# First input in one transfer, first weights sent for by ScalarE, and the second block joining at tile 12: the start of a fused attention and MoE kernel

## The chip, the cores and the metric

The kernel runs on one core of a Trainium2 chip. Its engines are TensorE (PE; PEld is its weight load), VectorE (DVE), ScalarE (ACT), GpSimd (POOL) and SyncE (SP, which here only issues transfers); transfers run on the core's 16 DMA engines. The metric is the device time of one execution in microseconds.

## The reference

Three layers run one after the other on 8192 tokens (two sequences of 4096) of 192 numbers. The first is an attention over the current and the six earlier tokens, with weights from a softmax over seven given numbers for each token and head; the others are two MoE layers with 2048 hidden columns.

```python
def _attn_ref(x, weight_gen):                  # x (2, 4096, 192), weight_gen (2, 4096, 8, 7)
    w = weight_gen - np.max(weight_gen, axis=-1, keepdims=True)
    w = np.exp(w)
    w = w / (np.sum(w, axis=-1, keepdims=True) + 1e-09)
    x_pad = np.concatenate([np.zeros((B, pad, D)), x], axis=1)
    idx = np.arange(S)[:, None] + np.arange(K)[None, :]
    x_unf = x_pad[:, idx, :].reshape(B, S, K, H, group)
    return np.einsum('bshk,bskhg->bshg', w, x_unf).reshape(B, S, D)

def _moe_ref(x, w_in, w_out):                  # w_in (192, 2048), w_out (2048, 192)
    h = np.maximum(x @ w_in, 0.0)
    return h * h @ w_out

def _moe2_ref(x, w_in, w_out):
    h = x @ w_in
    return (h * np.cos(h)) @ w_out
```

## The kernel before, in words

**Tiling.** The tokens are cut into 16 blocks of 512 (`N`), and the 2048 hidden columns of a layer into 16 tiles f of 128 (`NF`). A step (layer, block, tile) has five first products (L560), which make the tile `h`, and five second products (L577 to L583), which add it into two accumulators `acc`: ten matmuls with 512 columns each, since every fp32 operand is split into a high part and a low part that the PE can multiply at its faster rate. There are 512 steps and so 5120 products. Between the two kinds of product ACT and DVE (and POOL, later on) apply the layer's function to `h` and split it (`hi` L264, `lo` L271).

**Order of the steps.** The first layer's blocks 0 to 5 come first, then the two layers alternate by blocks. At the start block 0 runs alone for `ALONE` tiles (6); then blocks 0 and 1 alternate tile by tile, so that block 1's steps stand between the later tiles of block 0 (L538 to L541).

**Weights.** They arrive as fp32 and are split on the chip in pieces (`weight`, parts a and b for `w_in`, o for `w_out`): for each piece a load into a shared room (`wo_early` and others), an absolute value on ACT (L303), a scaled copy on POOL or ACT (L310), a sign mask on DVE (L313), a clamp on DVE or POOL (L315), a merge on DVE (L318), a sum on POOL (L320), then the copy to the high part (L264, L268) and the subtraction for the low part (L271). The names `wiAhi`, `wiAlo`, `wiB` and `wo` are the finished weights. The first layer's pieces are planned ahead of the step that needs them (`pace`).

**First block.** `load_x(0)` brings block 0's tokens as rows of 1920 numbers, a row for each partition, with the six tokens ahead of it: partitions 2 to 63 (62 rows) on SP's queue, 64 to 127 (64 rows) on ACT's; two short transfers fill partitions 0 and 1. `first_x1` then makes block 0's input for the MoE at once on PE: DVE multiplies a quarter of it with its seven weights (L441), PE sums the taps by seven matmuls with the identity (L482), DVE folds the last 64 columns in three additions (L487), PE transposes those (L493), and the sum is split (`xhi`, `xlo`). This is done four times, i = 0 to 3; the first two need the first half of the softmax (`wgen`, L402 to L414), the others the second.

**Other blocks.** POOL makes the four products (`pr`, L441), DVE reduces them (`at`, L454) and transposes them (L506), SP stores and reloads the result through DRAM (L512, L517), and it is split into `xhi` and `xlo` of that block, (0, 1) for block 1.

**What sets the order.** Every operation is recorded with the engines that could run it, a cost for each, what it reads and writes, and when it is due. `Order.issue` (L112 to L161) then hands them out greedily, engine by engine; the result is one fixed list of instructions for each engine, which the hardware runs in that order, an instruction waiting for what it needs. `SENT`, `RATE` and `SEEN` are the planner's own figures for a transfer, `since` a time before which it leaves an operation out of sight, `by` a time at which it is due, `behind` an operation that it is tied to. `WARM` matmuls with the identity (L700) run on PE before anything else.

Of the kernel before, what the change touches and what calls it, by code (L numbers as in the profile page):

```python
# [18 lines left out]
P = 128  # L19
# [4 lines left out]
LAG = 6  # L24
START = 18.0
LEAD = 6
ALONE = 6
WARM = 16


def bits(n):
# [24 lines left out]
class Order:  # L56
    WAIT = 0.14

    SENT, RATE, SEEN = 0.65, 360e3, 0.77

    MORE = {"dve": 0.6, "pool": 0.0, "act": 0.05}
    NEAR = 0.02
# [25 lines left out]
    def op(self, ways, fn, reads=(), writes=(), size=0, behind=None, by=1e9, over=(), since=0.0):  # L88
        o = Op()
        o.ways, o.fn, o.size = ways, fn, size  # L90
        o.late = self.SENT + size / self.RATE + self.SEEN if size else 0.0
        o.behind, o.by, o.since = behind, by, max(since, self.since)
        o.older, o.deps, o.after, o.n = set(over), set(), set(behind or ()), len(self.ops)
        for write, accesses in ((False, reads), (True, writes)):
            for a in accesses:
                b, key = a if isinstance(a, tuple) else (a, None)
                for p, w, k in b.log:
                    if (w or write) and (k is None or key is None or k == key):
                        o.deps.add(p)
                if b.log:  # L100
                    o.after.add(b.log[0][0])
                elif b.before is not None:
                    o.after.add(b.before.log[0][0])
                if b.older is not None:
                    o.older.add(b.older)
                b.log.append((o, write, key))
        o.deps.discard(o)
        o.after.discard(o)
        self.ops.append(o)
        return o  # L110
# [57 lines left out]
def dve(n, fast=False):  # L168
    return 0.069 + n / (1600 if fast else 900)
# [7 lines left out]
def conv_moe_kernel(  # L177
# [11 lines left out]
    B, S, D = x.shape  # L189
# [9 lines left out]
    DB = D - P  # L199
# [8 lines left out]
    w_in = [w.bitcast(U32) for w in (moe_w_in, moe2_w_in)]  # L208
# [5 lines left out]
    order = Order()  # L214
    op, buf = order.op, order.buf
# [5 lines left out]
    def const(shape, dtype, name):  # L221
        return Buf(None, tile=sb.tile(shape, dtype, name=name))

    def load(dst, out_fn, in_ap, size, key=None, reads=(), by=1e9, queue="sp"):
        op({queue: 0.45}, lambda e: eng[e].dma_start(out=out_fn(), in_=in_ap), reads=reads,
           writes=[(dst, key)], size=size, by=by)

    ident = const([P, P], F32, "ident")
    zero = const([P, 1], F32, "zero")
# [44 lines left out]
    def weight(m, part, c0, n):  # L274
        name = f"{part}{m}_{c0}"
        by = -99.0 if m == c0 == 0 and part != "o" else 1e9
        if m == 0:
            order.since = 3.0 if by < 0 else 5.0
        stage = lambda tag, n, shape: (
            order.lent(room[tag], tag + "0", f"{tag}{name}") if m == 0 else sbuf(shape, U32, tag, n, f"{tag}{name}"))  # L280
        raw = stage("raw", 2, [P, WC, 2])
        flat = lambda: raw.t.rearrange("p a b -> p (a b)")
        if part == "a":
            cols = n
            load(raw, lambda: flat()[:, 0:2 * n], w_in[m][0:P, 2 * c0:2 * (c0 + n)], P * n * 8, by=by)
        elif part == "b":

            cols = n // 2
            ap = w_in[m][P:D, 2 * c0:2 * (c0 + n)].rearrange("d (j k c) -> k d j c", k=2, c=2 * P)
            for k in range(2):  # L290
                load(raw, lambda k=k: flat()[k * DB:(k + 1) * DB, 0:n].rearrange("d (j c) -> d j c", c=2 * P),
                     ap[k], DB * n * 4, key=k, by=by)
        else:
            cols = n * D
            load(raw, lambda: flat()[:, 0:2 * n * D].rearrange("p (j d) -> p j d", j=n),
                 w_out[m][c0 * P:(c0 + n) * P, :].rearrange("(j p) d -> p j d", p=P), P * cols * 8)
# [64 lines left out]
    def load_x(b):  # L361
        rows = BS + PAD
        t = xc[b] = sbuf([P, rows, D], F32, "xc", 2, f"xc{b}")

        def rows_of(p0, p1, skip=0):
            ap = x_rows[b * N + p0 * BS - PAD + skip:b * N + p0 * BS + BS, :]
            return bass.AP(tensor=ap.tensor, offset=ap.offset, ap=[[BS * D, p1 - p0], [1, (rows - skip) * D]])


        p0 = -(-PAD // BS) if b * N % S == 0 else 0  # L370
        flat = lambda a, b, skip: t.t[a:b, skip:rows].rearrange("p r d -> p (r d)")
        if b:
            load(t, lambda: flat(p0, P, 0), rows_of(p0, P), P * rows * D * 4, key="all")
        else:
            for n, q in enumerate(((p0, P // 2), (P // 2, P))):
                load(t, lambda q=q: flat(*q, 0), rows_of(*q), P // 2 * rows * D * 4, key=f"all{n}", by=-100.0,
                     queue="act" if n else "sp")
        if p0:
            op({"pool": 1.0}, lambda e: nc.gpsimd.memset(t.t[0:p0, 0:PAD, :], 0.0), [], [(t, p) for p in range(1, p0)])
        for p in range(p0):  # L380
            skip = PAD - p * BS
            load(t, lambda p=p, skip=skip: flat(p, p + 1, skip), rows_of(p, p + 1, skip), 8192, key=p, by=1e9 if b else -100.0)
# [8 lines left out]
    exps = []  # L391
# [77 lines left out]
    def first_x1():  # L469
        t = [buf(ps, [P, N], F32, "h", 4, f"first{part}") for part in range(2)]  # L470
        for i in range(BS):
            if i < 2:
                pr = sbuf([P, K, D], F32, "pr", 2, f"pr0_{i}")
            else:
                pr = order.lent([pr0[:, i - 2]], f"pr{i}", f"pr0_{i}")
            twice = order.lent([twice0[:, i]], f"twice{i}", f"twice{i}")
            product(0, i, pr, ways={"dve": dve(K * D)})
            there = lambda part, i=i: t[part].t.rearrange("d (p i) -> d i p", i=BS)[:, i]

            def taps(e, pr=pr, there=there):  # L480
                for k in range(K):
                    nc.tensor.matmul(there(0), lhsT=pr.t[:, k, 0:P], rhs=ident.t, start=k == 0, stop=k == K - 1)  # L482
            op({"pe": 0.24 * K}, taps, [ident, (pr, 0)], [(t[0], i)])

            def fold(e, pr=pr, twice=twice):
                p = pr.t[:, :, P:D]
                add = lambda out, in0, in1: eng[e].tensor_tensor(out=out, in0=in0, in1=in1, op=ALU.add)  # L487
                add(p[:, 0:3], p[:, 0:3], p[:, 3:6])
                add(p[:, 0:2], p[:, 0:2], p[:, 2:7:4])
                add(twice.t, *(p[:, k].unsqueeze(1).to_broadcast([P, 2, DB]) for k in range(2)))  # L490
            op({"dve": dve(3 * DB) + 2 * dve(2 * DB)}, fold, [], [(pr, 1), twice])

            op({"pe": 0.24}, lambda e, twice=twice, there=there: nc.tensor.transpose(  # L493
                there(1), twice.t.rearrange("p q d -> p (q d)"), ident.t), [ident, twice], [(t[1], i)])
        for part in range(2):
            split((0, 0), part, t[part], True)
# [40 lines left out]

    two = steps[:ALONE]  # L538
    for f in range(NF - ALONE):
# [118 lines left out]
    for b in range(NB):  # L658
        when(final[0, b] + LAG + 1, take_x2, b)
        when(final[1, b] + LAG + 1, take_out, b)  # L660
        t = first[1, b]
# [3 lines left out]
        t = first[0, b]  # L665
        ago = lambda n: max(t - n, -1) if b > 1 else -1
        when(ago(NF + 8), load_x, b)
        if b % CB == 0:
# [4 lines left out]
            else:  # L673
                n = 14 + 9 * c
# [6 lines left out]
    t = first[1, 0]  # L681
# [69 lines left out]
```

## Time and profile before

| what | us |
|---|---|
| three runs | 1277.4, 1278.64, 1281.92 (median 1278.64) |
| the profiled execution | 1277.48 |
| its span, first to last instruction | 1274.5 |
| PE busy | 1196.8 |
| ACT busy | 1054.9 |
| DVE busy | 902.8 |
| POOL busy | 551.2 |

The span is what the trace covers; 2.98 us of the profiled execution lie around it. Busy is the time in which an engine had an instruction in hand; overlapping engines each count in full. A row of a timeline gives the start, the duration, the engine, the line and the operation, output from input, with the count at x; in brackets stands how long the engine was idle before it and what ended that.

### The profile page before, as it was taken

The numbers are of one execution on the slowest core, as the hardware profiler recorded it, in microseconds if no ns is written. First come the engines' busy times: TensorE is split into PE (matmuls) and PEld (weight loads), VectorE is DVE, ScalarE is ACT, GpSimd is POOL, SyncE is SP. The second block draws the span as 40 slices with busy tenths as digits, with TensorE's granted clock in tenths as the row PEclk, the third lists the DMA queues.
The fourth block names the chain that finished last, engine by engine and source line by source line (L and its number), as shares of the span: only waits on it lengthen the run. The fifth ranks groups of instructions, "written<-read, shape, count | busy, mean of one in ns | idle before, by whom it ended". The sixth has DMA issues, their size and how long they took to land.

```text
span 1274.5 us, 16270 instructions
## 1 busy us (share of the span) xinstructions
PE 1196.8 (94%) x5212; PEld 979.1 (77%) x5212; DVE 902.8 (71%) x1217; ACT 1054.9 (83%) x1992; POOL 551.2 (43%) x425
## 2 busy tenths in 40 slices
PE   4488999989999999999999999999999999999998
PEld 4367777778787887878788787878878888888886
DVE  5998879775958578585866758576674646777765
ACT  1486887869788797978879798888988979999996
POOL 3678465564615244260534526153332304444443
PEclk8689999999999999999999999999999999999999
DMA  4532435320212112021111202111020210111001
GB/s 115 154 96 67 133 109 166 113 69 21 80 30 69 25 31 79 10 72 31 56 46 28 74 9 69 34 37 27 24 47 9 54 30 13 30 30 30 13 7 19
DMA packets 91945, 68.67 MB, mean 54 GB/s; under 512 B 56020, under 2 KB 77268, under 8 KB 91860
## 3 DMA queue, kind: packets, MB, share of 16 engines
q1 hardware_dynamic: 91780, 67.16, 19.1%
q8 instruction: 40, 0.66, 0.2%
q10 hardware_dynamic: 80, 0.49, 0.2%
q14 instruction: 45, 0.37, 0.1%
HBM read 47.76 MB, written 19.86 MB: 53 GB/s over the span
## 4 chain that ended last, share of the span: by engine, by line
PE 50%; ACT 18%; DVE 14%; issue 5%; DMA 2%; POOL 1%; SPq 1%; DVEq 0%; ACTq 0%; POOLq 0%
PE h L560 25%; PE acc L579 5%; PE acc L577 5%; PE acc L578 5%; PE acc L582 5%; PE acc L583 5%; ACT hi L264 5%; DVE lo L271 4%; ACT rr L609 4%; ACT rr L610 4%; DVE g L612 2%; ACT kk L604 2%; DVE rr L607 2%; ACT g L598 2%; DVE at L454 1%
## 5 line engine op out<-in xcount | busy, mean ns | idle before, releaser
L271 POOL TENSOR_TENSOR lo<-g,hi 128x512 fp32r<-128x512 f32 x201 | 260.2, 1295 | 557.4 <-ACT hi L264 489.3
L271 DVE TENSOR_TENSOR lo<-g,hi 128x512 fp32r<-128x512 f32 x215 | 175.0, 814 | 157.1 <-ACT hi L264 147.5
L264 ACT ACTIVATE hi<-g 128x512 fp32r<-128x512 f32 x416 | 259.8, 625 | 1.9 <-DVE g L612 0.9
L607 DVE SCALAR_TENSOR_TENSOR rr<-kk,h 128x512 f32<-128x512 int32 x256 | 174.4, 681 | 90.0 <-ACT kk L604 90.0
L612 DVE TENSOR_TENSOR g<-h,rr 128x512 f32<-128x512 f32 x256 | 175.0, 684 | 38.6 <-POOL lo L271 26.8
L577 PE MATMUL acc<-hi,wo 128*128 128x512 f32 x512 | 200.3, 391 | 1.5 <-ACT wo L264 1.5
L578 PE MATMUL acc<-hi,wo 128*128 128x512 f32 x512 | 200.6, 392 | 1.0 <-DVE wo L271 1.0
L582 PE MATMUL acc<-lo,wo 128*128 128x512 f32 x512 | 200.4, 391 | 0.0
L579 PE MATMUL acc<-hi,wo 128*128 128x512 f32 x512 | 200.4, 391 | 0.0
L583 PE MATMUL acc<-lo,wo 128*128 128x512 f32 x512 | 200.2, 391 | 0.0
L594 ACT ACTIVATE rr<-h 128x512 f32<-128x512 f32 x256 | 150.7, 590 | 51.0 <-PE h L560 50.0
L609 ACT ACTIVATE rr<-rr 128x512 f32<-128x512 f32 x256 | 161.1, 629 | 27.7 <-DVE rr L607 27.4
L610 ACT ACTIVATE rr<-rr 128x512 f32<-128x512 f32 x256 | 161.2, 630 | 1.8
L604 ACT ACTIVATE kk<-h 128x512 int32<-128x512 f32 x256 | 151.1, 590 | 8.5 <-PE h L560 7.8
L598 ACT ACTIVATE g<-rr 128x512 f32<-128x512 f32 x160 | 100.7, 630 | 55.1 <-DVE lo L271 51.5
L441 POOL TENSOR_TENSOR pr<-xc,wgen_late 128x1344 f32<-128x1344 f32 x48 | 139.5, 2984 | 13.2 <-DVE at L454 11.8
L577 PEld LDWEIGHTS acc<-hi,wo 128*128 128x128 f32 x512 | 96.8, 189 | 22.1 <-ACT wo L264 1.9
L578 PEld LDWEIGHTS acc<-hi,wo 128*128 128x128 f32 x512 | 96.7, 189 | 21.6 <-DVE wo L271 1.3
L582 PEld LDWEIGHTS acc<-lo,wo 128*128 128x128 f32 x512 | 96.7, 189 | 20.3
L583 PEld LDWEIGHTS acc<-lo,wo 128*128 128x128 f32 x512 | 96.8, 189 | 20.1
L579 PEld LDWEIGHTS acc<-hi,wo 128*128 128x128 f32 x512 | 96.8, 189 | 20.0
L454 DVE TENSOR_REDUCE at<-pr 128x192 f32<-128x1344 f32 x60 | 92.3, 1539 | 0.0
(558 smaller groups left out, 2243.7 us busy)
## 6 DMA issues: line engine op xcount, KB each, us to landing
xc<-in_x_dram SPq DMA_DIRECT2D x14, 960.0 KB, 4.7
x2d<-x2a SPq DMA_DIRECT2D x16, 256.0 KB, 2.0
x<-x2d SPq DMA_DIRECT2D x32, 128.0 KB, 2.7
x<-x2d SPq DMA_DIRECT2D x16, 256.0 KB, 2.7
out_dram<-oa SPq DMA_DIRECT2D x64, 64.0 KB, 2.0
x1d<-xt SPq DMA_DIRECT2D x60, 64.0 KB, 1.8
x<-x1d SPq DMA_DIRECT2D x15, 256.0 KB, 2.7
x<-x1d SPq DMA_DIRECT2D x30, 128.0 KB, 2.6
```

The source lines that it names most:

```text
L264: nc.scalar.activation(out, in_, AF.Copy)
L271: eng[e].tensor_tensor(out=out, in0=in0, in1=in1, op=ALU.subtract)
L560: nc.tensor.matmul(h.t, lhsT=w.t[:, sl], rhs=v.t, start=n == 0, stop=n == len(ops) - 1)
L577: nc.tensor.matmul(o0.t, lhsT=w(0), rhs=hi.t, start=start, stop=False)
L578: nc.tensor.matmul(o1.t, lhsT=w(2), rhs=hi.t, start=start, stop=False)
L579: nc.tensor.matmul(o0.t, lhsT=w(1), rhs=hi.t, start=False, stop=False)
L582: nc.tensor.matmul(o1.t, lhsT=w(2), rhs=lo.t, start=False, stop=stop)
L583: nc.tensor.matmul(o0.t, lhsT=w(0), rhs=lo.t, start=False, stop=stop)
L607: op({"dve": dve(N)}, lambda e: nc.vector.scalar_tensor_tensor(out=r.t, in0=k.t, scalar=-TWO_PI, in1=h.t, op0=ALU.mult, op1=ALU.add), [k, ...
L609: op({"act": act(N)}, lambda e: nc.scalar.activation(r.t, r.t, AF.Abs), [], [r])
L610: op({"act": act(N)}, lambda e: nc.scalar.activation(r.t, r.t, AF.Sin, scale=-1.0, bias=math.pi / 2), [], [r], behind=exps if (b, f) == (0 ...
L612: op({"dve": dve(N)}, lambda e: nc.vector.tensor_tensor(out=g.t, in0=h.t, in1=r.t, op=ALU.mult), [h, r], [g])
```

## The change

The first input's 126 rows come in one transfer on SP, where there were two of 62 and 64 rows on two queues. The first pieces of the first layer's weights are issued on ACT's queue and tied to the first exponential. Blocks 0 and 1 alternate from tile 12 on instead of 6, which moves much in the lists of DVE, POOL and SP. Ten more warm-up matmuls are issued, and the planner's figures for a transfer, its cost of a fold and some `since` values change.

```diff
-ALONE = 6
-WARM = 16
+ALONE = 12
+WARM = 26
...
-    SENT, RATE, SEEN = 0.65, 360e3, 0.77
+    SENT, RATE, SEEN = 0.75, 300e3, 0.8
...
-    def load(dst, out_fn, in_ap, size, key=None, reads=(), by=1e9, queue="sp"):
+    def load(dst, out_fn, in_ap, size, key=None, reads=(), by=1e9, queue="sp", behind=None):
         op({queue: 0.45}, lambda e: eng[e].dma_start(out=out_fn(), in_=in_ap), reads=reads,
-           writes=[(dst, key)], size=size, by=by)
+           writes=[(dst, key)], size=size, by=by, behind=behind)
...
         by = -99.0 if m == c0 == 0 and part != "o" else 1e9
+
+        early = dict(queue="act", behind=exps[:1], by=by) if by < 0 else {}
         if m == 0:
-            order.since = 3.0 if by < 0 else 5.0
+            order.since = 0.0 if by < 0 else 6.5
...
-            load(raw, lambda: flat()[:, 0:2 * n], w_in[m][0:P, 2 * c0:2 * (c0 + n)], P * n * 8, by=by)
+            load(raw, lambda: flat()[:, 0:2 * n], w_in[m][0:P, 2 * c0:2 * (c0 + n)], P * n * 8, **early)
...
-                     ap[k], DB * n * 4, key=k, by=by)
+                     ap[k], DB * n * 4, key=k, **early)
...
-        if b:
-            load(t, lambda: flat(p0, P, 0), rows_of(p0, P), P * rows * D * 4, key="all")
-        else:
-            for n, q in enumerate(((p0, P // 2), (P // 2, P))):
-                load(t, lambda q=q: flat(*q, 0), rows_of(*q), P // 2 * rows * D * 4, key=f"all{n}", by=-100.0,
-                     queue="act" if n else "sp")
+        if b == 1:
+            order.since = 6.5
+        load(t, lambda: flat(p0, P, 0), rows_of(p0, P), P * rows * D * 4, key="all", by=1e9 if b else -100.0)
+        order.since = 0.0
...
-            op({"dve": dve(3 * DB) + 2 * dve(2 * DB)}, fold, [], [(pr, 1), twice])
+            op({"dve": 1.0}, fold, [], [(pr, 1), twice])
```

Line numbers from L280 to L371 are two higher after the change (L313 becomes L315, L318 becomes L320); the others named here stay.

The start of SP's list, as a piece of the difference; `xc` is a block's input, `wgen` the softmax weights, and the transfers are given as rows by columns:

```order
-L225 DMA wgen_99<-in_weight_gen_dram 128x224
-L225 DMA xc_101<-in_x_dram 62x1920
-L225 DMA xc_101<-in_x_dram 1x768
-L225 DMA xc_101<-in_x_dram 1x1536
-L225 DMA wgen_99<-in_weight_gen_dram 128x224
-L225 DMA xc_108<-in_x_dram 128x1920
-L225 DMA wgen_112<-in_weight_gen_dram 128x224
-L225 DMA wo_early<-in_moe_w_in_dram 128x512
-L225 DMA wo_early<-in_moe_w_in_dram 64x2x256 x2
-L225 DMA wgen_112<-in_weight_gen_dram 128x224
+L225 DMA wgen_109<-in_weight_gen_dram 128x224
+L225 DMA xc_111<-in_x_dram 126x1920
```

The 64-row half, which stood on ACT's queue, is gone; the first weights (128x512, and 64x2x256 twice) have left SP for ACT, and block 1's input (`xc_108`) goes down the list behind the weights that follow.

The list of DVE of the kernel before, from the third product of `first_x1` to the split of block 0's input, which the first product needs; `at1` is block 1's attention, `wo1_early` also the room in which `first_x1` works:

```order
L441 TENSOR_TENSOR wo1_early_72<-xc0_101,wgen0_99 128x1344 x2
...
L454 TENSOR_REDUCE at1_200<-pr1_0_174 128x192
L313 TENSOR_SCALAR wiB1_early_70<-wo1_early_72 128x256 x2
...
L318 SCALAR_TENSOR_TENSOR wiB1_early_70<-wiAlo1_early_68,wiB1_early_70 128x256 x2
L454 TENSOR_REDUCE at1_200<-pr1_1_198 128x192
L313 TENSOR_SCALAR wiB1_early_70<-wo1_early_72 128x384
L315 TENSOR_SCALAR wiAlo1_early_68<-wiAlo1_early_68 128x384
L271 TENSOR_TENSOR xlo0_(0, 0)_224<-first0_132,xhi0_(0, 0)_203 128x512
```

The same place after the change:

```order
L441 TENSOR_TENSOR wo1_early_72<-xc0_111,wgen0_109 128x1344
...
L487 TENSOR_TENSOR wo1_early_72<-wo1_early_72 128x128
L315 TENSOR_SCALAR wiB1_early_70<-wo1_early_72 128x256 x2
L320 SCALAR_TENSOR_TENSOR wiB1_early_70<-wiAlo1_early_68,wiB1_early_70 128x256 x2
L315 TENSOR_SCALAR wiB1_early_70<-wo1_early_72 128x384
L271 TENSOR_TENSOR xlo0_(0, 0)_215<-first0_139,xhi0_(0, 0)_202 128x512
```

Block 1's two reductions have moved behind the split, and so has the second half of the softmax (which stood ahead of the rows shown). On POOL block 1's four products stand as instructions 15 to 18 before, right behind five short weight passes, and as 28, 29, 34 and 35 after.

The list of PE where block 1's first tile joins, before (`xlo0_(0, 1)` is block 1's input, `xlo0_(0, 0)` block 0's):

```order
L560 MATMUL h7_412<-xlo0_(0, 1)_370,wiAhi0_65 128x512
L560 MATMUL h7_412<-xhi0_(0, 1)_359,wiAlo0_67 128x512
L560 MATMUL h7_412<-xhi0_(0, 1)_359,wiAhi0_65 128x512
L560 MATMUL h7_412<-xlo1_(0, 1)_400,wiB0_69 128x512
L560 MATMUL h7_412<-xhi1_(0, 1)_388,wiB0_69 128x512
L560 MATMUL h8_427<-xlo0_(0, 0)_224,wiAhi0_65 128x512
```

and after:

```order
L560 MATMUL h13_646<-xlo0_(0, 1)_583,wiAhi0_65 128x512
L560 MATMUL h13_646<-xhi0_(0, 1)_577,wiAlo0_67 128x512
L560 MATMUL h13_646<-xhi0_(0, 1)_577,wiAhi0_65 128x512
L560 MATMUL h13_646<-xlo1_(0, 1)_636,wiB0_69 128x512
L560 MATMUL h13_646<-xhi1_(0, 1)_627,wiB0_69 128x512
L560 MATMUL h14_657<-xlo0_(0, 0)_215,wiAhi0_65 128x512
```

Block 1's first tile moved from the 8th step, behind 45 products, to the 14th, behind 115. Step h14 is tile 13 of block 0: it stands behind 120 products here and behind 170 in the list before, where it is step h20.

## Rows read from the trace of the kernel before

**Rows 1.** The page: busy us of each engine, share of the span, instructions.

```profile
PE 1196.8 (94%) x5212; PEld 979.1 (77%) x5212; DVE 902.8 (71%) x1217; ACT 1054.9 (83%) x1992; POOL 551.2 (43%) x425
```

**Rows 2.** Windows by stage: from and to, length, busy us of each engine (instructions).

```profile
core 0: us, PE busy (x) PEld busy (x) DVE busy (x) ACT busy (x) POOL busy (x), PEclk, DMA share, GB/s
0.00:17.60 17.60, 5.57 (x32) 5.38 (x32) 2.21 (x8) 1.87 (x3) 1.70 (x7) 0.84 0.53 138
17.60:45.60 28.00, 9.43 (x60) 8.35 (x60) 27.62 (x34) 5.94 (x14) 16.58 (x11) 0.74 0.41 123
45.60:113.50 67.90, 56.20 (x200) 41.41 (x201) 64.07 (x93) 47.47 (x100) 49.37 (x57) 0.87 0.29 85
113.50:160.40 46.90, 46.12 (x201) 37.30 (x201) 39.19 (x52) 39.75 (x78) 28.30 (x23) 1.00 0.46 140
160.40:1274.50 1114.10, 1079.46 (x4721) 886.67 (x4719) 769.71 (x1034) 959.90 (x1801) 455.23 (x329) 1.00 0.17 45
```

**Rows 3.** Timeline of DVE, 17 to 67 us: start, duration, instruction.

```profile
17.61 3.03 DVE L441 TENSOR_TENSOR pr<-xc,wgen 128x1344 f32<-128x1344 f32 x2 [11.94 <-DMA xc<-in_x_dram]
...
20.55 0.38 DVE L402 TENSOR_REDUCE mx<-wgen 128x32 f32<-128x224 f32 x1
...
24.71 0.39 DVE L414 TENSOR_TENSOR wgen<-wgen,sx 128x224 f32<-128x224 f32 x1
...
26.49 3.92 DVE L441 TENSOR_TENSOR wo_early<-xc,wgen 128x1344 f32<-128x1344 f32 x1
30.34 3.37 DVE L487 TENSOR_TENSOR wo_early<-wo_early 128x192 f32<-128x192 f32 x3
33.62 1.54 DVE L454 TENSOR_REDUCE at<-pr 128x192 f32<-128x1344 f32 x1
35.08 2.90 DVE L313 TENSOR_SCALAR wiB_early<-wo_early 128x256 uint32<-128x256 uint32 x2
37.90 0.99 DVE L487 TENSOR_TENSOR wo_early<-wo_early 128x192 f32<-128x192 f32 x3
...
41.21 2.76 DVE L315 TENSOR_SCALAR wiAlo_early<-wiAlo_early 128x384 f32<-128x384 f32 x1
...
50.62 0.34 DVE L315 TENSOR_SCALAR wiAlo_early<-wiAlo_early 128x384 f32<-128x384 f32 x1
50.89 1.07 DVE L506 STREAM_TRANSPOSE xt<-at 128x512 f32<-128x512 f32 x1
51.81 0.27 DVE L313 TENSOR_SCALAR wiB_early<-wiB_early 128x256 uint32<-128x256 uint32 x1
...
66.74 0.99 DVE L271 TENSOR_TENSOR xlo_(0, 1)_400<-x,xhi_(0, 1)_388 128x512 fp32r<-128x512 f32 x1
```

**Rows 4.** Timeline of PE: block 0's first product, and its tile 13.

```profile
45.66 0.79 PE L560 MATMUL h<-xlo_(0, 0)_224,wiAhi 128*128 128x512 f32 x1 [6.23 <-DVE wiB_early L318]
...
104.90 0.39 PE L560 MATMUL h<-xlo_(0, 0)_224,wiAhi 128*128 128x512 f32 x1
```

**Rows 5.** Windows of three shorter stretches, with the columns of rows 2.

```profile
2.00:10.00 8.00, 4.94 (x31) 4.75 (x30) 2.15 (x7) 0.61 (x3) 0.30 (x1) 1.00 1.01 252
...
10.00:17.00 7.00, 0.00 (x0) 0.00 (x0) 0.00 (x0) 0.00 (x0) 0.00 (x0) 0.63 0.14 51
...
104.90:113.50 8.60, 7.04 (x31) 5.53 (x30) 7.83 (x7) 5.02 (x10) 6.42 (x4) 1.00 0.00 0
```

**Rows 6.** DMA view, start and 28 to 36: count, KB, us to landing.

```profile
xc<-in_x_dram SPq DMA_DIRECT2D x1, 465.0 KB
...
xc<-in_x_dram SPq DMA_DIRECT2D x1, 960.0 KB, 4.8
```

**Rows 7.** Timeline of SP's queue: the first input's issues.

```profile
1.19 1.36 SPq L225 DMA_DIRECT2D xc<-in_x_dram  x3
```

**Rows 8.** Timeline of POOL, 21 to 33 us.

```profile
21.73 0.42 POOL L310 TENSOR_SCALAR wiAhi_early<-wo_early 128x256 uint32<-128x256 uint32 x1 [19.43 <-DMA wo_early<-in_moe_w_in_dram]
...
25.24 7.67 POOL L441 TENSOR_TENSOR pr<-xc,wgen 128x1344 f32<-128x1344 f32 x2 [0.39 <-DVE wgen L414]
```

## The prediction

> **What bounds the kernel now.** I read the page first, then the windows by stage, then the timelines of the stages in which TensorE is short of work. On the page PE is busy nearly the whole span [rows 1], so a change at the start can only win what PE waits there. The windows say how much that is [rows 2]. In the last and longest stretch 4721 matmuls take 1114.1 us; a matmul with 512 columns takes 0.227 us at the full clock (46.90 us for 201, near enough, in the stretch before it, 0.233 with its small gaps), so that stretch is a queue of products with 4% of gaps. From 113.5 on there is little to win. Up to 113.5 only 200 products have started, 45.4 us worth: **68 us are lost in the head**, and that is where every part of the change lies.
>
> The head has three parts. Up to 17.6 little but the warm-up and the first half of the softmax runs. VectorE then starts, having stood idle for 11.94 us for the first input [rows 3]. From 17.6 to 45.6 DVE is busy 27.62 of 28.00 us, and the first product starts only at 45.66 [rows 2, 4]. From 45.6 to 113.5 DVE is still busy 64.07 of 67.9 us while PE has gaps. So up to 113.5 the kernel goes at the pace of **one list on DVE that begins when the first input lands**; PE gets a tile whenever DVE has made its weights. The last place where PE waits on this list is tile 13 of block 0 at 104.90 [rows 4]; from there to 113.5 it issues its last 30 products with small gaps [rows 5].
>
> Why does the input land so late? Up to 10 us the 16 DMA engines are full and move 252 GB/s, but from 10 to 17 us their busy share is 0.14, that is 2.2 of 16, at 51 GB/s [rows 5]: the 62-row half (465 KB) trickles through about two engines after all else has landed. A 128-row transfer of 960 KB, sent alone, lands in 4.8 us [rows 6].
>
> **The change, part by part.**
>
> *One transfer instead of two halves.* Issue stays at 1.19 us on SP [rows 7]. I read the trace so: a transfer's rows are dealt out in equal shares, 62 = 2 x 31 gives two shares, 128 gives sixteen, so 126 = 14 x 9 gives fourteen. Bounds: not before 1.2 + 4.8 = 6.0 (the 128-row price), and, if everything now asked for early (1.8 MB of input, first weights and weight_gen) is in its way at 252 GB/s from 2 us on, 9.1. I take 6.8, near the lower end, since the first weights are now sent for only behind the first exponential, on ACT's queue. DVE's list starts 17.6 - 6.8 = **10.8 us earlier** (bounds 8.5 to 11.6).
>
> *First weights from ACT's queue.* Three issues of about 0.5 us each on ACT. What stands behind them on ACT is the first pass over these very weights, so they delay nothing. In the kernel before these weights were issued on SP behind the first input, and POOL first got one at 21.73 after 19.43 us of waiting [rows 8]; now they should land near 10, when DVE's folds are under way. Price nothing; if that cover went (landing after about 17), the first product would move one for one.
>
> *Block 1 behind tile 12.* This moves DVE and POOL work, as the order shows. Ahead of the first product DVE loses two reductions of block 1 (1.54 each, 3.1), the second half of block 0's softmax (six instructions from 20.55 to 25.10, 2.3 us busy together, the first and the last shown) and four collisions with POOL's products of block 1. [...] One product takes 3.92 us where the two at 17.61 take 1.52 each; three folds 3.37 where three take 0.99; two sign passes 2.90 where one takes 0.27; one clamp 2.76 where one takes 0.34 [rows 3, 8]. Together 12.95 where 3.39 would do: **9.5 us**. So of 28.05 us 28.05 - 9.5 - 3.1 - 2.3 = 13.1 remain, plus up to 1.5 for short weight passes of POOL that fall beside DVE: the first product starts at 6.8 + 13.1 = 19.9 to 21.4, some 24 us earlier.
>
> That is not the gain. The reductions, the softmax half and the collisions move behind the first product, and the weights for 16 tiles must still be made on the same list: DVE has 124 instructions ahead of the 200th product before and 123 after. What decides is the last place at which PE waits. Tile 13 of block 0 stands behind 170 products before and behind 120 after (50 products of block 1 have gone behind it), and behind 116 DVE instructions before and 107 after. So DVE's term at tile 13 is:
> - list starts 10.8 earlier;
> - nine instructions fewer ahead: four subtractions of the mean size of the stretch (64.07/93 = 0.69) and five weight passes of 0.34, 4.5 us (bounds nine times 0.27, 2.4, and nine times 0.69, 6.2);
> - collisions: upper bound all 9.5; lower bound 2.5, if block 1's four products collide as before, later, and only the six POOL instructions that go to ACT (68 on POOL up to the 200th product, 62 after) are saved at 0.42 [rows 8]. I take 7, as if one of the four collided again: now weight passes of POOL stand between them, and DVE's reductions and its subtractions of finished tiles stand beside them.
>
> Tile 13 at 104.9 - 10.8 - 4.5 - 7 = **82.6**. From there 80 products are left to the 200th, 80 x 0.227 = 18.2, so the 200th starts at **100.8 instead of 113.5: -12.7**. DVE's list alone would be through earlier (6.8 + 95.9 - 7 = 95.7), so PE, not DVE, sets this end; that is what caps the gain.
>
> *Block 1 itself.* Before, its chain from the transposes to its low half takes 15.9 us (50.89 to 66.74 [rows 3]). After, its transposes stand at row 82 of DVE's list and its first product behind 115 others, about 81 us. Its x loads stand behind weight loads on SP. I price it at nothing, at most 4 us, with the alone tiles of block 0 as cover.
>
> *Warm-up.* Before, 32 instructions take 5.57 us [rows 2]; 20 more take 2.1 to 3.5 and end before 10.5. Only the taps of the first stage queue behind them, and these go on until DVE's last fold, at 6.8 + 4 x 1.52 + 4 x 0.99 = 16.8. Nothing. Their use, if any, is a higher granted clock in the first products: in 17.6 to 45.6 it was 0.74, where PE issued only taps [rows 2].
>
> *Planner constants.* They move loads and the choice of engine; all I count of them is in the orders above.
>
> *After the 200th product.* The same 4720 products follow with the same gaps: nothing, with -4 to +3 for later loads that move.
>
> Sum on the profiled execution: 1277.5 - 12.7 = 1264.8. The median shown stands 1.2 above that execution, so **1265.9 us**. A difference within 0.3% (3.8 us) can't be told from none.
>
> **The rivals.**
> - *More is won.* No collision comes back (-2.5) and the later loads bring up to 4: 1265.9 - 2.5 = 1263 down to 1256 with the other bounds at their good ends. For it: PE has 42 us of gaps after 160 [rows 2]. Against: nothing in the change touches them.
> - *Less is won,* 1271 to 1274.8: block 1 comes late by its 4 us, and the collisions return.
> - *Block 0 alone starves PE.* Twelve tiles ask for weights at twice the rate, and block 1's work returns to DVE in the same stretch: nothing but the transfer's 10.8 is kept at tile 13. 104.9 - 10.8 = 94.1, + 18.2 = 112.3, -1.2: 1277.4. For it: DVE is busy 64 of 68 us where this happens [rows 2]. Against: the orders count nine instructions fewer.
> - *The transfer changes nothing.* The input lands at 17.6 all the same, and the rest is kept: 104.9 - 11.5 = 93.4, + 18.2 = 111.6, -1.9: 1276.8. For it: the same bytes cross the same 16 engines. Against: a share of 0.14 [rows 5]. [...]
> - *Slower: the one transfer trickles too.* Place: SP's 126-row transfer. If 126 rows also go through two engines, 968 KB at 51 GB/s take 19.0 us and land at 20.2 or later; at the 29 GB/s of the whole 465 KB (476 thousand bytes in 16.4 us) at 34.6. In the middle DVE starts 9.8 later: tile 13 at 104.9 + 9.8 - 11.5 = 103.2, the 200th at 121.4, +7.9: 1286.6. It decides (over 0.3% slower) from a landing at 23.3 on. For it: 126 is no more a multiple of 16 than 62 is. Against: it has the divisors 14 and 9. [...] No transfer of 126 rows is in the trace.
>
> **How the numbers follow.** Forecast 0.68, with its own range 1261 to 1271 (the landing +2.3, the collisions and later loads 4 either way, not all together). More won 0.12, less won 0.05, block 0 starves 0.06, transfer nothing 0.04, trickles 0.05. Faster by over 0.3%: 0.68 + 0.12 + 0.05 = 0.85; same 0.06 + 0.04 = 0.10; slower 0.05. 1256 to 1273 leaves out the last three and half of "less".
>
> **What would show it.** DVE's first product at about 6.8; no stretch with a DMA share near 0.14 ahead of it; the first product at 20 to 21.4; DVE without gap up to some 96; PE's last wait for a weight near 82.6; the 200th product at 100.8; and beyond it the same lag as before. Wrong it is if DVE starts later than 9.1, if PE still waits for weights after product 120, if the first product of block 1 waits for its x, or if what is ahead at the 200th product is not ahead at the end.

## The result, and the profile after

The changed kernel takes 1262.26 us (median of 4 runs, 1260.3 to 1265.73) where the kernel before takes 1278.02 (4 runs, 1277.21 to 1281.92): a ratio of 0.9874, 95% interval 0.9844 to 0.9904. That is 15.8 us less, clear of noise; 1265.9 was forecast. The profiled execution took 1262.56 us, with a span of 1260.7.

The windows by stage of the changed kernel, with the columns of [rows 2]; the edges are its own stages (input landed, first product, tile 13 of block 0, 200th product):

```profile
core 0: us, PE busy (x) PEld busy (x) DVE busy (x) ACT busy (x) POOL busy (x), PEclk, DMA share, GB/s
2.00:9.50 7.50, 7.09 (x51) 6.90 (x50) 2.15 (x7) 0.62 (x3) 0.30 (x1) 1.00 0.82 239
...
9.50:23.20 13.70, 8.97 (x60) 8.40 (x60) 13.34 (x23) 3.81 (x9) 7.93 (x10) 0.88 0.63 210
23.20:81.90 58.70, 38.36 (x121) 26.23 (x122) 57.20 (x87) 39.62 (x88) 40.49 (x40) 0.83 0.39 119
81.90:100.00 18.10, 18.10 (x81) 15.01 (x80) 12.31 (x16) 14.58 (x27) 16.43 (x13) 1.00 0.00 0
100.00:160.00 60.00, 57.26 (x250) 46.42 (x249) 52.95 (x64) 48.55 (x92) 37.08 (x22) 1.00 0.47 144
160.00:1260.70 1100.70, 1069.51 (x4673) 879.74 (x4671) 761.97 (x1030) 951.70 (x1788) 437.78 (x315) 0.99 0.17 44
```

The stretch of [rows 5] in which the DMA engines trickled at a share of 0.14 is gone; the input lands at 9.5, and DVE is busy 13.34 of 13.70 and then 57.20 of 58.70 us, so its list still runs almost without a hole up to tile 13. From there to 100.0 PE is busy all the time. What is left behind 160 has the gaps that it had.

DVE's timeline up to the first product, which answers to [rows 3]:

```profile
9.59 3.24 DVE L441 TENSOR_TENSOR pr<-xc,wgen 128x1344 f32<-128x1344 f32 x2 [4.04 <-DMA xc<-in_x_dram]
...
18.71 1.92 DVE L487 TENSOR_TENSOR wo_early<-wo_early 128x192 f32<-128x192 f32 x6
20.55 0.49 DVE L315 TENSOR_SCALAR wiB_early<-wo_early 128x256 uint32<-128x256 uint32 x2
...
22.43 0.68 DVE L271 TENSOR_TENSOR xlo_(0, 0)_215<-first,xhi_(0, 0)_202 128x512 fp32r<-128x512 f32 x1
```

and PE's, answering to [rows 4], with the first product, the two longest waits of the head and its last:

```profile
23.25 0.47 PE L560 MATMUL h<-xlo_(0, 0)_215,wiAhi 128*128 128x512 f32 x1 [2.24 <-DVE xlo_(0, 0)_215 L271]
...
38.83 0.76 PE L560 MATMUL h<-xlo_(0, 0)_215,wiAhi 128*128 128x512 f32 x1 [4.76 <-DVE lo L271]
...
55.08 0.79 PE L560 MATMUL h<-xlo_(0, 0)_215,wiAhi 128*128 128x512 f32 x1 [6.20 <-DVE lo L271]
...
81.31 0.50 PE L560 MATMUL h<-xlo_(0, 1)_636,wiB 128*128 128x512 f32 x1 [0.85 <-DVE xlo_(0, 1)_636 L271]
```

Six folds take 1.92 us together and two sign passes 0.49: the waits that [rows 3] show at these instructions are away from here. DVE's list from its start to the first product shrank from 28.05 to 13.7 us. But PE still waits long later on, now for the subtractions of finished tiles (`lo`), which release the four PSUM tiles `h`.

The place where the kernel gains, counted from PE's rows in both traces (the 200th product is the one with 200 others ahead of it):

| start of | before | after | difference |
|---|---|---|---|
| DVE's first product | 17.61 | 9.59 | -8.0 |
| first product on PE | 45.66 | 23.25 | -22.4 |
| tile 13 of block 0 | 104.90 | 81.89 | -23.0 |
| 200th product | 113.56 | 100.03 | -13.5 |
| last product (5120th) | 1267.71 | 1254.06 | -13.6 |

The gain is complete at the 200th product and only carried on from there. The profiled executions themselves lie 14.9 apart (1.1 of it around the spans) and the medians 15.8; the interval of the ratio reaches from 12 to 20 us.

### The profile page after: what moved, and what is told of

The parts are those of the page before. It is cut to its first block, busy times and chain, and to the rows that moved or that the text cites. A ratio compares the mean times of both kernels' runs of the same rounds, so it can differ in the third digit from the quotient of the medians.

```text
span 1260.7 us, 16319 instructions
## 1 busy us (share of the span) xinstructions
PE 1199.9 (95%) x5232; PEld 983.3 (78%) x5232; DVE 900.0 (71%) x1224; ACT 1060.1 (84%) x2004; POOL 541.4 (43%) x406
## 4 chain that ended last, share of the span: by engine, by line
PE 64%; DVE 16%; ACT 13%; issue 3%; POOL 1%; DMA 1%; SPq 0%; DVEq 0%; ACTq 0%; POOLq 0%
PE h L560 33%; PE acc L579 6%; PE acc L578 6%; PE acc L577 6%; PE acc L582 6%; PE acc L583 6%; ACT hi L264 3%; ACT rr L609 3%; DVE lo L271 3%; ACT rr L610 3%; DVE g L612 2%; DVE at L454 2%; ACT kk L604 2%; DVE rr L607 1%; DVE xt L506 1%
## 5 line engine op out<-in xcount | busy, mean ns | idle before, releaser
L271 POOL TENSOR_TENSOR lo<-g,hi 128x512 fp32r<-128x512 f32 x197 | 255.4, 1296 | 556.9 <-ACT hi L264 518.9
L271 DVE TENSOR_TENSOR lo<-g,hi 128x512 fp32r<-128x512 f32 x219 | 178.7, 816 | 159.2 <-ACT hi L264 148.9
L264 ACT ACTIVATE hi<-g 128x512 fp32r<-128x512 f32 x416 | 259.8, 624 | 3.4 <-DVE g L612 1.7
L578 PEld LDWEIGHTS acc<-hi,wo 128*128 128x128 f32 x512 | 96.8, 189 | 23.2 <-DVE wo L271 3.0
L579 PEld LDWEIGHTS acc<-hi,wo 128*128 128x128 f32 x512 | 96.9, 189 | 20.1
L454 DVE TENSOR_REDUCE at<-pr 128x192 f32<-128x1344 f32 x60 | 92.4, 1539 | 0.3 <-POOL pr L441 0.3
```

The costliest lines, as they stand in the source:

```text
L264: nc.scalar.activation(out, in_, AF.Copy)
L271: eng[e].tensor_tensor(out=out, in0=in0, in1=in1, op=ALU.subtract)
L578: nc.tensor.matmul(o1.t, lhsT=w(2), rhs=hi.t, start=start, stop=False)
L579: nc.tensor.matmul(o0.t, lhsT=w(1), rhs=hi.t, start=False, stop=False)
```

## The experiments

All ratios are to the kernel before on the same chip, where its median was 1280.6 us for runs 1 to 4 and 1278.8 for the others; the changed kernel has 0.9874.

**1 and 2. How the first input is cut.** In the changed kernel the one transfer is replaced by two, on SP and ACT; the cut is all that differs between the two.

```diff
-        load(t, lambda: flat(p0, P, 0), rows_of(p0, P), ...)
+            for n, q in enumerate(((p0, P // 2), (P // 2, P))):      # e1: 62 and 64 rows
+            for n, q in enumerate(((p0, 58), (58, P))):              # e2: 56 and 70 rows
+                load(t, lambda q=q: flat(*q, 0), rows_of(*q), ..., queue="act" if n else "sp")
```

> The changed kernel with the first input in two halves again (62 rows on SP, 64 on ACT), all else as changed. Theory of the prediction, with the landing that the changed kernel measured (9.59 us): the 62-row half again lands at 17 us or later, with a stretch of DMA share below 0.2 ahead of it; DVE's list starts some 8 us later, and the 200th product comes 6 to 9 us later than at 100.0: 1268 to 1271 us. Rival (the transfer changes nothing, the gain is all from block 1's place and the queues): DVE starts by 11 us as in the changed kernel, 1261 to 1264.

> The changed kernel with the first input in two transfers on two queues, cut so that both have 14 as a divisor of their rows: 56 rows on SP, 70 on ACT. If the number of equal shares of the rows decides (prediction): no trickle, DVE starts at 8.5 to 10.5 us, 1260 to 1265 us. Rival (two transfers on two queues are what made it late, whatever their rows): DVE starts at 14 us or later, 1266 to 1271.

Measured: 62 and 64 rows 1271.09 us (0.9931, 0.9904 to 0.9957); 56 and 70 rows 1261.96 (0.9872, 0.9843 to 0.9901). DVE's first product with 62 and 64 rows, and the window of 10 to 17 us with the columns above:

```profile
20.12 3.25 DVE L446 TENSOR_TENSOR pr<-xc,wgen 128x1344 f32<-128x1344 f32 x2 [14.58 <-DMA xc<-in_x_dram]
...
10.00:17.00 7.00, 0.00 (x0) 0.00 (x0) 0.00 (x0) 0.44 (x1) 0.83 (x2) 0.74 0.12 35
```

and with 56 and 70 rows, with the window of 5 to 10 us:

```profile
8.72 3.25 DVE L446 TENSOR_TENSOR pr<-xc,wgen 128x1344 f32<-128x1344 f32 x2 [2.25 <-DMA xc<-in_x_dram]
...
5.00:10.00 5.00, 5.00 (x37) 4.84 (x36) 2.59 (x5) 0.11 (x2) 0.03 (x1) 1.00 0.93 201
```

With 62 and 64 rows the trickle is back (a share of 0.12 is 1.9 of the 16 engines), DVE starts 10.5 us later than in the changed kernel and the 200th product comes at 110.34, 10.3 later: one for one. That is a little more than the 6 to 9 expected. With 56 and 70 rows, still two transfers on two queues, DVE starts 0.9 us earlier than with one. So it isn't the number of transfers but their row counts: 62 rows are slow, and 56, 64, 70, 126 and 128 are not (the 64-row half landed 9.4 us after its issue in the kernel before, with the engines full). The traces of before and after give the shares that the prediction read: the landing of the 62-row half is recorded in 2 parts (at 16.6 and 17.4 us), that of 126 rows in 14, and those of the 64-row half and of a block's 128 rows in 16; 62 and 126 rows have one more record, some 0.6 us behind the issue. A transfer of 126 rows stood in the trace of before too, against what the prediction says: the input of the second sequence, issued at 267.34. It landed 6.3 us after that, and from 269 to 271 its DMA share was 0.88, which is 14.1 of 16. For the cut into 56 and 70 rows only the landing and the share of 0.93 are shown, not the parts. Two transfers in place of one changed little with 56 and 70 rows (8.72 against 9.59, within 1 us); with 62 and 64 the pair is 10 us slower than the one.

**3. Block 1 from tile 6 again.** In the changed kernel:

```diff
-ALONE = 12
+ALONE = 6
```

> The changed kernel with block 1 joining at tile 6 again. Theory of the prediction: the first product waits again for two reductions, a softmax half and collisions with POOL (first product near 35 to 38 us), tile 13 of block 0 again stands behind 170 products; of the 13.5 us that the changed kernel gained at the 200th product the transfer's 8 stay: 1266 to 1270 us. Rival (block 0 alone is worth nothing, or starves PE): 1258 to 1264.

Measured: 1270.71 us (0.9925, 0.9901 to 0.9948), just above the expected range. PE's first product, and DVE's instructions ahead of it that last longest:

```profile
41.29 0.79 PE L560 MATMUL h<-xlo_(0, 0)_232,wiAhi 128*128 128x512 f32 x1 [10.68 <-ACT wiAhi L264]
```

```profile
16.77 5.39 DVE L441 TENSOR_TENSOR wo_early<-xc,wgen 128x1344 f32<-128x1344 f32 x2
22.09 3.37 DVE L487 TENSOR_TENSOR wo_early<-wo_early 128x192 f32<-128x192 f32 x3
...
26.83 3.25 DVE L487 TENSOR_TENSOR wo_early<-wo_early 128x192 f32<-128x192 f32 x3
...
31.86 3.12 DVE L320 SCALAR_TENSOR_TENSOR wiB_early<-wiAlo_early,wiB_early 128x256 uint32<-128x256 uint32 x2
```

Collisions with block 1's four products stand there again, at almost the prices of [rows 3], two of them at other instructions. The first product is 18 us later than in the changed kernel, which is more than I expected (35 to 38), and what it waits for is ACT's copy of the first weights. Their sum on POOL was done at 36.37, but in ACT's list the copy stands behind the absolute value of a later piece (L305), which waits 4.51 us for its load and starts at 40.39; the copy follows at 40.84. At the 200th product 3.1 us of that are left (103.12), and 7.0 more are lost from there to the 600th (207.59 against 197.54), so that the time is not explained by the head alone; what is late there I left open.

**4. First weights on SP.** In the changed kernel:

```diff
-        early = dict(queue="act", behind=exps[:1], by=by) if by < 0 else {}
+        early = dict(by=by)
```

> The changed kernel with the first weights issued on SP again, not tied to the exponential. Theory of the prediction: their issue is worth nothing while they land before about 17 us; with no trickle on SP they land by 13: 1261 to 1265 us. Rival (ACT's queue is what brought the weights ahead): POOL gets its first weight after 17 us, first product at 27 or later, 1266 to 1270.

Measured: 1261.46 us (0.9865, 0.9839 to 0.9892); DVE starts at 9.66, POOL gets its first weight at 10.15, the first product comes at 23.21. The queue is worth nothing once nothing trickles on SP. (While the 62 rows trickle it is: POOL gets its first weight at 14.01 in run 1, from ACT's queue, and at 21.73 in [rows 8], from SP's.)

**5 and 6. The two main parts alone, in the kernel before.** One transfer (the new `load_x`, all else as before), and block 1 from tile 12 (the input in two halves, all else as before):

```diff
-            for n, q in enumerate(((p0, P // 2), (P // 2, P))):                     # e5
-                load(t, lambda q=q: flat(*q, 0), rows_of(*q), ...)
+        load(t, lambda: flat(p0, P, 0), rows_of(p0, P), P * rows * D * 4, key="all", by=1e9 if b else -100.0)
...
-ALONE = 6                                                                            # e6
+ALONE = 12
```

> The kernel before with the first input in one transfer, all else as before. Theory of the prediction: DVE starts 7 to 9 us earlier, and as long as DVE's list sets the pace to tile 13 the 200th product follows it: 1269 to 1272 us. Rival (the start is swallowed, since the weights or block 1 come late): 1275 to 1279.

> The kernel before with block 1 joining at tile 12, all else as before. Theory of the prediction: nine instructions fewer and the collisions are saved ahead of tile 13, 11.5 us by the prediction's terms and 15 by what the changed kernel measured, less the 9.4 us that 50 more products take behind it: 1.9 to 5.4 us are won, 1273 to 1277 us. Rival (block 0 alone starves PE): 1278 or more.

Measured: one transfer 1271.7 us, 0.9939 (0.9915 to 0.9962), 5 to 11 us won; tile 12 1271.65 us, 0.995 (0.9933 to 0.9968), 4 to 9 us won. One transfer starts DVE at 9.80, 7.8 earlier, and the 200th product comes at 106.01, 7.5 earlier: the start is passed on almost whole, and nothing swallows it. With tile 12 the 200th product comes at 109.13, 4.4 earlier, inside the 1.9 to 5.4 of the theory; the time is 1.4 us better than the expected range, which its interval still meets. The two together, 0.0061 + 0.0050 = 0.0111 of the time, are close to the 0.0126 of the whole change, within the intervals: the other edits have little left to give.

**7 and 8. Warm-up and planner figures.** In the changed kernel:

```diff
-WARM = 26                                                                            # e7
+WARM = 16
...
-    SENT, RATE, SEEN = 0.75, 300e3, 0.8                                              # e8
+    SENT, RATE, SEEN = 0.65, 360e3, 0.77
-            op({"dve": 1.0}, fold, [], [(pr, 1), twice])
+            op({"dve": dve(3 * DB) + 2 * dve(2 * DB)}, fold, [], [(pr, 1), twice])
```

> The changed kernel with 16 warm-up matmuls in place of 26. Theory of the prediction: nothing, 1261 to 1264 us, the 200th product within 1 us of 100.0. Rival (they hold the granted clock up until the taps): the granted clock from 9.5 to 23.2 falls from 0.88 to below 0.8, and the first product is 1 to 3 us later, 1263 to 1266.

> The changed kernel with the planner's old figures for transfers and for a fold. Theory of the prediction: they only move instructions; the head to the 200th product stays within 2 us: 1260 to 1265 us. Rival (part of the gain is from the better order that they give): 200th product 3 us later or more, 1265 to 1270.

Measured: 1262.48 us (0.9871) and 1263.55 (0.9875), the 200th product at 99.56 and 100.32. Neither is worth anything that can be measured. The granted clock from 9.5 to 23.2 was 0.98 with 16 warm-up matmuls and 0.88 with 26, the reverse of the rival's claim.

**9. PE not idle in two of its waits.** In the changed kernel idle matmuls on the identity, into a PSUM tile that isn't in use yet, stand ahead of steps 4 and 8 (counted from 0):

```diff
+    FILL = {4: 18, 8: 24}
+            for n in range(fill):
+                nc.tensor.matmul(idle.t[:, n % BS * P:(n % BS + 1) * P], lhsT=ident.t, rhs=ident.t, start=True, stop=True)
             for n, (w, v) in enumerate(ops):
```

> The changed kernel with 18 idle matmuls ahead of step 4 and 24 ahead of step 8, in the two longest waits of PE in the head (4.76 us at 38.8, 6.20 us at 55.1), so that PE isn't idle in them; nothing else moves. Products after those waits took 0.43 us instead of 0.227, some 35 of the first 200, 6 us together. Theory 1 (DVE's list sets the pace of the head, PE catches up in the next wait): products 20 to 70 run at the full clock, but tile 13 and the 200th product are at most 2 us earlier: 1259 to 1263 us. Theory 2 (the low granted clock is a bound of its own): the 200th product 4 to 6 us earlier, 1256 to 1259.

Measured: 1263.49 us (0.9887, 0.9864 to 0.9910), the 200th product at 101.25, 1.2 later than in the changed kernel. PE's rows around the two fillings:

```profile
30.82 4.18 PE L564 MATMUL idle<-ident 128*128 128x128 f32 x36
...
38.76 0.47 PE L566 MATMUL h<-xlo_(0, 0)_215,wiAhi 128*128 128x512 f32 x1 [2.61 <-DVE lo L271]
...
49.87 5.90 PE L564 MATMUL idle<-ident 128*128 128x128 f32 x48
55.52 0.48 PE L566 MATMUL h<-xlo_(0, 0)_215,wiAhi 128*128 128x512 f32 x1
...
61.48 0.80 PE L583 MATMUL acc<-hi,wo 128*128 128x512 f32 x1 [3.43 <-ACT wo L264]
```

The first filling misses its place: the wait of 4.76 us lies ahead of step 5. Ahead of step 4 the changed kernel waits only 1.59 us, so that step starts 2.1 us later here (34.76 against 32.63), and 2.61 us of the longer wait stay. The second fills the wait of 6.20 us, and the product behind it starts 0.4 us later. The ten products behind it run at 0.23 us where they took 0.43, but the next wait, for `wo`, is 1.2 us longer and ends at 61.48, almost where it ended (61.92 in the changed kernel). So in this place the low clock is not the bound; PE only arrives sooner at what isn't ready.

More the run doesn't show. Behind that wait the granted clock is 0.50 (61.4 to 67.0), and products take 0.43 again up to 71.0, where they took 0.23 from 66.4 on in the changed kernel. Of the first 200 products 24 took 0.43, against 25 in the changed kernel (the expectation had some 35): the low clock was moved, not removed. The 4 to 6 us of theory 2 aren't there, and the time is just above the range of theory 1; what the head would take with no product at the low clock stays open.

**10. Block 1's products taken from POOL.** In the changed kernel they are replaced by copies on ACT:

```diff
+            if b == 1:
+                nc.scalar.activation(t, xc[b].t[:, i:i + K, :], AF.Copy)
+                return
```

> The changed kernel with block 1's four products replaced on ACT by plain copies of the input (the weighting of block 1's tokens is left out, so its output is not the reference's), so that POOL runs none of them. Theory (DVE's wait beside POOL's long products is a term of the head): the 8.9 us that DVE's instructions last longer beside them go, and tile 13 and the 200th product come 4 to 8 us earlier, 1255 to 1260 us; ACT has 4.8 us more to do. Rival (those collisions are hidden now, or ACT takes over as the bound): 200th product within 2 us of 100.0 or later, 1261 or more.

Measured: 1254.3 us (0.9810, 0.9792 to 0.9828), 0.7 below the expected range; the 200th product comes at 94.64, 5.4 earlier than in the changed kernel, and tile 13 at 75.29, 6.6 earlier (behind 115 products here, not 120). Up to the 200th product DVE's instructions last 15.8 us longer than at least, by the count of the next section, against 22.4 in the changed kernel. So the collisions with these four instructions are a term of the head; the rival falls. The run also takes 11.0 us of work from POOL, and what that is worth by itself it doesn't separate. What it removes is what the change had left in place, not what the change saved. Another 3 us are won beyond the 200th product, which I can't put down to one place: the lists behind it differ. The wait of 6.20 at 55.08 in the changed kernel is this term at work. DVE's and POOL's timelines of the changed kernel in that place:

```profile
46.41 3.71 DVE L317 TENSOR_SCALAR wiAlo_early<-wiAlo_early 128x384 f32<-128x384 f32 x2
50.03 2.91 DVE L271 TENSOR_TENSOR wiAlo<-wiB_early,wiAhi 128x384 fp32r<-128x384 f32 x1
...
54.34 0.68 DVE L271 TENSOR_TENSOR lo<-h,hi 128x512 fp32r<-128x512 f32 x1
```

```profile
47.04 5.53 POOL L441 TENSOR_TENSOR pr<-xc,wgen 128x1344 f32<-128x1344 f32 x2
```

Two clamps (0.34 each elsewhere, [rows 3]) and one subtraction take 6.6 us beside two products of POOL, and the subtraction that frees PE's tile stands right behind them, to end at 55.02, just ahead of PE's product.

**11 and 12. Block 1 from tile 9, and from tile 16.** `ALONE = 9` and `ALONE = 16` in the changed kernel.

> The changed kernel with block 1 joining at tile 9, between 6 (1270.7 us) and 12 (1262.3). Theory: tile 13 of block 0 stands behind some 145 products and block 1's work is still ahead of part of the weights: 1263 to 1268 us. Rival (only the first product's list matters, which is free of block 1 from some tile on): as with 12, 1261 to 1263.

> The changed kernel with block 1 only after all 16 tiles of block 0. Theory: no products of block 1 lie between the last tiles of block 0 while their weights are made, so PE waits for the weights of tiles 13 to 15, and nothing more is saved on DVE: 200th product 0 to 4 us later than at 100.0, 1262 to 1267 us. Rival (the later the better): 1256 to 1260.

Measured: 9 gives 1272.14 us (0.9947, 0.9927 to 0.9966), 16 gives 1262.77 (0.9879, 0.9859 to 0.9899). The first is worse than expected and no better than 6; neither the theory's numbers nor the rival's hold. POOL's and ACT's timelines with 9 show why:

```profile
22.65 5.37 POOL L441 TENSOR_TENSOR pr<-xc,wgen 128x1344 f32<-128x1344 f32 x2 [3.48 <-PE first L493]
27.93 1.56 POOL L322 TENSOR_TENSOR wiB_early<-wiB_early,wiAhi_early 128x256 uint32<-128x256 uint32 x2
```

```profile
31.13 0.58 ACT L404 ACTIVATE wgen<-wgen 128x448 f32<-128x448 f32 x1 [4.12 <-DVE wgen L403]
...
32.48 0.40 ACT L264 ACTIVATE wiAhi<-wiB_early 128x256 fp32r<-128x256 f32 x1
```

POOL's list there has block 1's products ahead of the sums of the very first weights (L322), which are so finished at 29.5 instead of 23.1. Another 3 us are lost on ACT: its copy of these weights (L264), for which the first product (32.9) waits, stands behind the exponential of another softmax (L404), which waits 4.12 us for DVE. It is the planner's lists, not the number of tiles as such, and they jump: the way to the first product is free of block 1 with 12 and 16, not with 6 and 9. With 16 the 200th product comes at 103.18, 3.2 later than with 12, with PE waiting for weights, as expected, and the time can't be told from that with 12.

## Why the prediction was right

The direction, the place and the size were right: 12.7 us at the 200th product were forecast, 13.5 measured, 1265.9 us against 1262.26. That the sum comes so close is partly luck: one term fell short by 2.8 us, and the others gave 3.5 more than was forecast. The terms at tile 13 of block 0 can be measured apart. For DVE's instructions from its first product to that tile I added up what each lasts at least (the 5th percentile of its operation and shape over all fourteen traces), and what it lasted beyond that (all but 0.6 us before and 0.2 after with an instruction of POOL beside it):

```
us                              before   after   difference   forecast
list starts                      17.6      9.6      -8.0        -10.8
instructions (119 and 109)       62.8     56.4      -6.4         -4.5
longer than that                 28.6     20.8      -7.8         -7
gaps less overlaps               -4.1     -4.9      -0.8          0
tile 13 of block 0              104.9     81.9     -23.0        -22.3
to the 200th (30, 80 products)    8.7     18.1      +9.5         +9.6
200th product                   113.56   100.03    -13.5        -12.7
```

- *Landing of the input.* The step that was mis-sized: 6.8 was taken, 9.5 measured, outside the bounds of 6.0 to 9.1. Up to 9.5 the DMA engines moved 239 GB/s at a share of 0.82; in 7.5 us that is the 1.8 MB of input, weight_gen and first weights, which I had counted at the upper end and then not taken. So the upper bound was nearly the truth. That the input would land near 6.8 without the others is not shown: no run holds them back. The 6.8 means 5.6 us from issue to landing; the 126 rows of the second sequence, with next to nothing beside them, took 6.3 before and 6.6 after, which would be 7.5 and 7.8 here.
- *List shorter.* Ten instructions instead of nine, and one of them a reduction of 1.54: the price of a mean instruction was too small a price for what moved. At 6.4 it lies just above its bound of 6.2, 1.9 us the other way, and by chance makes up for most of the landing.
- *Collisions.* 7 was taken between 2.5 and 9.5, and 7.8 measured, but the mechanism was another. The prediction had block 1's collisions gone but for one. All four products stand ahead of tile 13 again, later, and beside them DVE loses 8.9 us against 9.6 before, here and in the rows under run 10:

```profile
32.61 2.63 DVE L271 TENSOR_TENSOR wiB<-wiB_early,wiB 64x256 fp32r<-64x256 f32 x1
...
35.80 2.27 DVE L271 TENSOR_TENSOR wiAlo<-wiB_early,wiAhi 128x384 fp32r<-128x384 f32 x1
```

```profile
32.32 5.43 POOL L441 TENSOR_TENSOR pr<-xc,wgen 128x1344 f32<-128x1344 f32 x2
```

  This is the case for which the prediction had its lower bound of 2.5. Of the 7.8, 3.8 are from two later products of POOL (at 96.28 and 102.70 before), which no longer start ahead of tile 13, and 2.9 from POOL's short instructions (14.6 before, 11.7 after), which the lower bound had at 2.5. So the size of this term was luck. Run 10 shows that the 8.9 still count.
- *Tile 13 as the last wait of PE.* Right in time, not in kind: tile 13 comes at 81.89 and PE doesn't wait afterwards up to the 200th product, but what ends last ahead of it is block 1's input (0.85 us at 81.31) and `wo` at 77.45, and the longest wait is for the release of a PSUM tile at 55.08. The sum holds since all three stand on DVE's list.
- *Its own signs of being wrong.* Two of four came true: DVE starts at 9.59, later than 9.1, and block 1's first product waits for its x. The price of nothing for block 1 was 0.85 us short; x itself was there, its high part done at 79.06, and the low part waited for DVE's list until 80.31. DVE also has gaps from 81.9 on (12.31 busy of 18.10), where none was forecast up to 96. The two others did not: PE waits for no weight between 81.9 and 160, and what is ahead at the 200th product is ahead at the end.
- *Cap by PE:* 80 products in 18.1 us, 18.2 forecast.
- *First product:* 19.9 to 21.4 forecast, 23.25 measured; with the landing put right (2.8) it is 22.7 to 24.2.
- *First weights' queue, warm-up, planner figures at nothing:* runs 4, 7 and 8 show it.
- *Rivals:* the trickle of one transfer and "the transfer changes nothing" fall with runs 1, 2 and 5; "block 0 starves PE" with run 6.

## What to carry to other kernels

Where one in-order list makes nearly everything that PE eats, a start that comes earlier is passed on whole (7.5 of 7.8 us in run 5, 10.3 of 10.5 lost in run 1), and a foreign instruction in that list costs its own time and what it draws in (12.95 us instead of 3.39 beside POOL's products in [rows 3]); look for both before PE's waits. Count an early transfer's landing by all bytes issued up to then, not by its own: here that gave 9.1 where 9.5 was measured. And a transfer's row count is a tuning knob: the same 126 rows cut as 62 and 64 instead of 56 and 70 cost 9 us here. A sum that comes out right doesn't vouch for its terms; only the terms measured one by one do.

## What the runs showed of the hardware

- A VectorE instruction beside GpSimd's long product is not always delayed. In the traces of before and after 52 reductions (L454) had such a product beside them and took 1.53 to 1.55 us, their usual price (5th to 95th percentile), while the subtractions of two SBUF tiles, the clamps and the sign passes took up to 3.1 us instead of 0.3 to 0.7. The reductions have one input, and so have the clamps and the sign passes; what sets them apart no run here shows.
- The 62-row half of the first input got slower when the first weights were no longer queued behind it on SP: 17.6 us before, 20.1 in run 1, with a DMA share of 0.12. From ACT's queue these weights were under way at the same time and landed 10.2 and 14.8 us after their issue (5.2 and 5.4 in run 2); whether that is what slowed the half is not shown.
- The granted clock was lower behind PE's wait of 6.2 us than with that wait filled. The windows behind it, in the changed kernel and in run 9:

```profile
55.00:66.40 11.40, 8.60 (x19) 6.13 (x20) 10.64 (x20) 6.27 (x15) 4.61 (x7) 0.65 0.56 191
```

```profile
55.50:61.40 5.90, 2.55 (x13) 1.80 (x11) 5.84 (x10) 4.12 (x10) 0.11 (x1) 0.96 0.65 234
```

  Inside the first window the clock was 0.50 from 55.0 to 59.4 and from 63.0 to 66.2, and products started 0.43 us apart there; where it was 1.00, from 81.9 to 100.0, 80 products took 18.1 us, 0.23 each. With the wait filled the mean was 0.96. It won nothing: the next wait took it up, and behind that one the clock was down at 0.50.
- The faster rate at which PE takes the split operands is seen beside the warm-up. In the changed kernel the 26 warm-up matmuls, fp32 with 128 columns, are 52 records, 0.11 us apart from 5.0 to 8.8 us at a granted clock of 1.00: 0.22 us for a matmul of 128 columns, where a product of 512 columns takes 0.23.
